# A planner that is given a duration for TensorE's changes of kind, and a preference for the kind that ran last

## The chip, the cores and the metric

The kernel runs on one core of a Trainium2 chip. Five engines work side by side, each through its own list of instructions in order: TensorE (PE in the profile; PEld is its weight load), VectorE (DVE), ScalarE (ACT), GpSimd (POOL) and SyncE (SP), which issues the DMAs. The metric is the device time of one execution in microseconds (us); lower is better.

## The reference

Three layers follow each other. Attention works on chunks of 64 tokens; its output is 2304 tokens of 512 numbers. A gated layer with an RMS norm and a layer of four experts follow.

```python
scores = scale * q_c @ k_c.T            # batch 4, 8 heads, 9 chunks of 64 x 64
attn = exp(scores - max); attn = attn / (sum(attn) + 1e-9)
x = attn @ v_c                          # -> 2304 x 512
xn = x / sqrt(mean(x * x) + 1e-6) * rms_g
x = (silu(xn @ w_gate) * (xn @ w_val)) @ w_out          # 512 -> 1536 -> 512, weights in float64
out = sum over e of p[:, e] * (relu(x @ w1[e]) @ w2[e]) # 4 experts, 512 -> 1024 -> 512
```

## The kernel before

The kernel does not issue its work in the order of the code. Each piece is added to a `Plan` as a node: the engine or engines that can do it, a duration, what it needs, which buffers it takes and gives, and a rank. `Plan.run` then makes the list: 90 passes of `forward`, which simulates the engines and always places the node that can start first (of those within 0.05 us on one engine, the one with the lower rank), and `backward`, which sets every rank to the latest start that still meets the end. When three passes bring nothing, the best ranks are taken with random noise (SEED, NOISE). The order of the best pass is written out; the planned times themselves do not reach the chip, only the order on each engine and the buffers. First ranks are made from due times, which start at `T0`; the first step of a weight conversion (`c1` in `converted`) also may not start before its rank (`after`), which is the due time less 8 us.

Tokens are in 18 tiles of 128, in blocks of 4, 4, 4, 4 and 2 tiles. `attention` does for each tile: loads of q, k and v (SyncE, L515), four TensorE transposes of q and as many of k (L552), copies to SBUF as qT and kT (ScalarE L561 or VectorE L563), the scores as 64-wide matmuls (`scores`, node s2, L582), maximum, subtraction and exponent (VectorE L601, L606, ScalarE L619), transposes of e (s3, L628), the values as 64-wide matmuls (`values`, s4, L657, into the one "av" bank), division, norm, transposes of x (s5, L716), and the split of x into a high and a low part (xh, xl). Each group of transposes has the planned duration 0.436 us and each group of 64-wide matmuls 1.2.

The gate and value weights come as float64 words in loads of 512 KB (`load_raw`, L772) and are converted by a chain that starts on ScalarE (`c1`, L792). The wide matmuls (128 x 128 x 512) of the first two weight columns (`proj`, L1141) run beside the attention of later tiles. Behind them come chains of seven products over pairs of blocks (L1287), then the output layer and the experts (L1684, L1876), with wide matmuls throughout. In `load_qkv` and `load_raw` the planned duration of an issue is 1.25 us for q, k or v and 1.6 for raw weights, and the transfer is planned at 2.2 or 2.0 us behind it.

Of the kernel before, what the change touches and what calls it, by code (L numbers as in the profile page):

```python
# [19 lines left out]
class Plan:  # L20
# [3 lines left out]


    PASSES = 90
    SEED = 10
    NOISE = 0.5
    LATENCY = 0.2
    MARGIN = 0.3  # L30

    def __init__(self):
        self.free_at = {}
# [13 lines left out]
    def add(self, eng, cost, emit, needs=(), takes=(), rank=0.0, lag=0.0, table=None, after=0.0, port=None):  # L47

        n = Node()
        n.engs = {eng: cost} if isinstance(eng, str) else eng  # L50
        n.emit, n.takes, n.rank, n.lag, n.table, n.after = emit, takes, rank, lag, table, after
        n.port = len(n.engs) > 1 and "Pool" in n.engs or eng == "Pool" if port is None else port
        n.needs = [x for x in needs if x is not None]
        n.gives = []
        n.alone = True
        n.users = []
        n.then = None
        n.end = None
        n.seq = len(self.nodes)
        n.open = len(n.needs)  # L60
        for x in n.needs:
            x.users.append(n)
        self.nodes.append(n)
        return n
# [13 lines left out]
    def run(self):  # L78


        first = {r: [list(x) for x in v] for r, v in self.res.items()}
        best, stalled = None, 0
        rng = random.Random(self.SEED)
        for k in range(self.PASSES):
            end = self.forward(first)
            stalled += 1
            if best is None or end < best[0] - 1e-6:
                best, stalled = (end, self.order, [n.rank for n in self.nodes]), 0
            if end < 1e8 and stalled < 3:
                self.backward()  # L90
            else:
                stalled = 0
                for n, r in zip(self.nodes, best[2]):
                    n.rank = r + rng.uniform(-self.NOISE, self.NOISE)
        for _, _, eng, n, ids in sorted(best[1], key=lambda x: x[:2]):
            n.ids = ids
        self.order = best[1]
        held = None
        for _, _, eng, n, ids in sorted(best[1], key=lambda x: x[:2]):
            n.emit(eng, *ids)  # L100
            if n.port and eng == "DVE":
                held = self.last()
            elif n.port and eng == "Pool" and held is not None and n.alone:
                self.behind(self.last(), held)
                held = None

    def forward(self, first):
# [1 line left out]
        self.res.update({r: [list(x) for x in v] for r, v in first.items()})  # L109
        self.state.clear()  # L110
        self.free_at, self.ready, self.order = {}, {}, []
        self.table, self.port_free, self.giver = None, 0.0, None
        for n in self.nodes:
            n.open, n.end, n.after_buffer = len(n.needs), None, []
        for n in self.nodes:
# [3 lines left out]
        while left:  # L119
            best = None  # L120
            for eng, ready in self.ready.items():
                cand = None
                for n in ready:
                    s = self.start_of(n, eng)
                    k = (s, n.rank, n.seq)
                    if cand is None:
                        cand = (k, n)
                    elif s < cand[0][0] - EPS or (s < cand[0][0] + EPS and k[1:] < cand[0][1:]):
                        cand = (k, n)
                if cand and (best is None or cand[0][0] < best[0]):  # L130
                    best = (cand[0][0], eng, cand[1])
            s, eng, n = best
            if s > 1e8:
                return 1e9
            cost = n.engs[eng]
            if n.table:
                if self.table != n.table:
                    cost += 1.28
                self.table = n.table
# [16 lines left out]
            for r, owner, k in n.gives:  # L156
                i = owner.ids[k]
                if callable(r):
                    r = r(i)
# [10 lines left out]
    def backward(self):  # L170
# [17 lines left out]
        for _, _, eng, n, _ in sorted(self.order, key=lambda x: (x[0] + x[3].cost, x[1]), reverse=True):  # L188
            t = late.get(n, end) - n.lag
# [9 lines left out]
                if x is not None:  # L199
                    late[x] = min(late.get(x, 1e9), s)  # L200
        for n in self.nodes:
            n.rank = n.late

    def make_ready(self, n):
        lat = self.MARGIN if "PE" in n.engs else self.LATENCY
# [14 lines left out]
def tile_attention_moe_moe2(  # L220
# [37 lines left out]
    NS = 6  # L258


    T0 = 36.0
    STRETCH = 1.3
    LEAD = 8.0
    HOLD = 0.0
# [266 lines left out]
    def attention(grp):  # L531
# [10 lines left out]
        for i in grp:  # L542
# [4 lines left out]
            for nm in "qk":  # L547
# [18 lines left out]
                tr = norm  # L566
                n = add("PE", 0.436, lambda e, a, b, f=transpose: f(e, a), needs=[ld[nm]], takes=["a", nm + "T"], rank=rank(i, 18))
                norm[nm, i] = n
                n.gives.append((nm, ld[nm], 0))
                c = add({"ACT": 0.6, "DVE": 0.69}, 0, copy, needs=[n], rank=rank(i, 17))  # L570
                c.gives.append(("a", n, 0))
# [16 lines left out]
                    tiles["ee", i] = at_p.tile([P, ng * H, CH], F32, tag=etag, name="e")  # L588

            s2 = add("PE", 1.2, scores, needs=[cp["q"], cp["k"]], takes=["a"] + (["e"] if i == key else []), rank=rank(i, 16))  # L590
            s2.gives += [("qT", norm["q", i], 1), ("kT", norm["k", i], 1)]
            if i == key:
                e_node = s2
# [29 lines left out]
        for n_, i in enumerate(grp):  # L623
# [8 lines left out]

            s3 = add("PE", 0.436, transpose_e, needs=[ex] + s3s, takes=["a", "eT"], rank=rank(i, 10))
            s3s.append(s3)
            if i == grp[-1]:
                s3.gives.append(("e", e_node, 1))

# [23 lines left out]
                tiles["xps", i] = ps  # L661

            s4 = add("PE", 1.2, values, needs=[ce, first[i]["v"]], takes=["av", "xs"], rank=rank(i, 8))
            s4.gives += [("eT", s3, 1), ("v", first[i]["v"], 0)]

            def total(_, i=i):
# [50 lines left out]
                tiles["xtps", i] = ps  # L717

            s5 = add("PE", 0.436, transpose_x, needs=[sl], takes=["a"], rank=rank(i, 3))
            s5.gives.append(("xs", s4, 1))  # L720

            def high(_, i=i):
# [46 lines left out]
    def load_raw(key, src, shape, dt, rank):  # L769
# [3 lines left out]
            tiles["raw", key] = t  # L773

        ld = add("SP", 1.6 if dt == I32 else 1.4, load, needs=[prev_ld[0]], takes=["raw"], rank=rank - 4, lag=2.0)
        prev_ld[0] = ld
        return ld

# [1529 lines left out]
```

## Time and profile before

| | |
|---|---|
| median of 3 runs | 1215.2 us (1212.56 to 1216.45) |
| profiled execution | 1215.69 us, span 1213.9 us |
| TensorE busy | 1196.7 us of the span (99%) |
| VectorE, ScalarE, GpSimd busy | 956.7, 593.9, 229.8 us |
| DMA | 227.00 MB, 187 GB/s on average |

The span goes from the first to the last instruction; the profiled execution's time also holds what lies around it. In the timeline a row merges instructions of one line that follow each other: start, the time up to the last one's end, line, tiles, shapes, count, and in brackets the idle time before it and what ended it. TensorE's matmuls overlap, so the pace of its groups is read from one start to the next. PEclk is the granted clock as a share of 2.4 GHz.

### The profile page before, as it was taken

What the parts mean: (1) busy time and instruction counts of PE and PEld (TensorE: products, weight loads), DVE (VectorE), ACT (ScalarE), POOL (GpSimd) and SP (SyncE); (2) the same over time, 40 slices, a digit from 0 to 9 for tenths busy, and PEclk for the clock granted to TensorE, in tenths of its full rate; (3) what the DMA queues carried; (4) which work ended last, traced back from release to release, by engine and by line L of the source; (5) the groups of instructions that cost most, each with busy time, mean ns of one, the idle gap of its engine ahead of it and who ended that gap; (6) DMA issues with size and microseconds to landing.
All of it is one profiled execution on the core that took longest, in us unless ns stands there. A gap on an engine that the chain in (4) does not pass through costs nothing.

```text
span 1213.9 us, 18543 instructions
## 1 busy us (share of the span) xinstructions
PE 1196.7 (99%) x6950; PEld 1015.5 (84%) x6950; DVE 956.7 (79%) x1416; ACT 593.9 (49%) x948; POOL 229.8 (19%) x175
## 2 busy tenths in 40 slices
PE   8899999999999999999999999999999999999998
PEld 7778888888888888888888888888788888888887
DVE  4888978888869689987888888888997466766577
ACT  5757544554647645455444444545535433342333
POOL 0132122211220021320332323323200101111001
PEclk9999999999999999999999999999999999999999
DMA  9973245545544772665465563754675755546553
GB/s 188 204 169 96 75 133 189 195 156 181 194 173 153 256 245 90 235 218 202 142 246 186 196 215 130 256 202 152 239 242 196 259 192 181 205 169 242 183 178 117
DMA packets 159662, 227.00 MB, mean 187 GB/s; under 512 B 66956, under 2 KB 102868, under 8 KB 159572
## 3 DMA queue, kind: packets, MB, share of 16 engines
q1 hardware_dynamic: 159572, 225.82, 56.1%
q8 instruction: 55, 0.90, 0.3%
q14 instruction: 35, 0.29, 0.1%
HBM read 137.66 MB, written 88.12 MB: 186 GB/s over the span
## 4 chain that ended last, share of the span: by engine, by line
PE 76%; DVE 4%; DMA 1%; ACT 0%; issue 0%; POOL 0%; SPq 0%; DVEq 0%; ACTq 0%
PE yps L1876 33%; PE hps L1684 25%; PE hps L1287 8%; PE hps L2112 4%; PE yr L2156 3%; PE hps L1416 1%; PE yo L1494 1%; DVE xa L1591 1%; DVE ha L1803 1%; PE ot L2042 1%; DMA raw<-in_moe_w_gate_dram 1%; DMA raw<-in_moe_w_val_dram 0%; DVE acc L1604 0%; DVE xx L1604 0%; DVE acc L1907 0%
## 5 line engine op out<-in xcount | busy, mean ns | idle before, releaser
L1876 PE MATMUL yps<-ha,w 128*128 128x512 f32 x1848 | 426.0, 390 | 0.6 <-DVE ha L1803 0.6
L1876 PEld LDWEIGHTS yps<-ha,w 128*128 128x128 f32 x1848 | 345.3, 188 | 72.1 <-DVE ha L1803 1.4
L1684 PE MATMUL hps<-xa,w 128*128 128x512 f32 x1344 | 313.9, 390 | 0.9 <-DVE w L946 0.6
L1684 PEld LDWEIGHTS hps<-xa,w 128*128 128x128 f32 x1344 | 250.0, 188 | 52.5 <-DVE w L946 1.0
L1803 DVE TENSOR_TENSOR ha<-hs,ha 128x1024 fp32r<-128x1024 f32 (+1 forms) x126 | 148.9, 1195 | 30.3 <-ACT ha L1797 30.0
L1797 ACT ACTIVATE ha<-hs 128x1024 fp32r<-128x1024 f32 (+1 forms) x126 | 119.2, 961 | 103.5 <-PE yps L1876 56.4
L1820 POOL TENSOR_TENSOR hs<-hs 128x1024 f32<-128x1024 f32 (+1 forms) x31 | 67.8, 2186 | 324.4 <-DVE ha L1803 284.5
L939 ACT ACTIVATE w<-raw 128x512 fp32r<-128x512 f32 x128 | 77.5, 627 | 81.4 <-DVE raw L953 30.5
L946 POOL TENSOR_TENSOR w<-raw,w 128x512 fp32r<-128x512 f32 x49 | 68.6, 1409 | 237.9 <-ACT w L939 81.2
L1907 DVE TENSOR_TENSOR acc<-acc,yps 128x512 f32<-128x512 f32 x128 | 85.1, 682 | 31.6 <-PE yps L1876 31.1
L1697 ACT ACTIVATE hps<-hps 128x512 f32<-128x512 f32 x64 | 37.3, 583 | 114.2 <-PE hps L1684 111.7
L1287 PE MATMUL hps<-xh,w 128*128 128x512 f32 x232 | 77.1, 390 | 0.0
L1890 ACT ACTIVATE yps<-yps 128x512 f32<-128x512 f32 x88 | 51.1, 581 | 44.7 <-PE yps L1876 35.3
L1745 DVE SCALAR_TENSOR_TENSOR hs<-hps,pb 128x512 f32<-128x512 f32 x96 | 64.9, 685 | 4.5 <-PE hps L1684 3.4
L1287 PE MATMUL hps<-xs,w 128*128 128x512 f32 x264 | 64.8, 389 | 0.0
L946 DVE TENSOR_TENSOR w<-raw,w 128x512 fp32r<-128x512 f32 x79 | 58.9, 767 | 5.8 <-ACT w L939 5.5
L953 DVE TENSOR_TENSOR raw<-raw 128x256 f32<-128x256 f32 x121 | 51.4, 425 | 14.2 <-POOL w L946 9.8
L1803 DVE TENSOR_TENSOR ha<-hl,ha 128x1024 fp32r<-128x1024 f32 x42 | 50.7, 1220 | 13.3 <-ACT ha L1797 13.2
L1797 ACT ACTIVATE ha<-hl 128x1024 fp32r<-128x1024 f32 x42 | 44.3, 1058 | 29.8 <-PE yps L1876 16.1
L1705 DVE TENSOR_TENSOR hps<-hps,p 128x512 f32<-128x512 f32 x32 | 22.3, 698 | 46.0 <-ACT hps L1697 46.0
L1287 PEld LDWEIGHTS hps<-xs,w 128*128 128x128 f32 x264 | 49.5, 188 | 10.4
L1287 PEld LDWEIGHTS hps<-xh,w 128*128 128x128 f32 x232 | 43.6, 188 | 8.9
(166 smaller groups left out, 1791.8 us busy)
## 6 DMA issues: line engine op xcount, KB each, us to landing
w<-wk SPq DMA_DIRECT2D x112, 512.0 KB, 4.5
wk<-w SPq DMA_DIRECT2D x110, 512.0 KB, 4.9
raw<-in_moe_w_dram SPq DMA_DIRECT2D x32, 512.0 KB, 4.8
hl<-sd SPq DMA_DIRECT2D x48, 256.0 KB, 3.1
sd<-s SPq DMA_DIRECT2D x38, 256.0 KB, 2.1
wk<-w SPq DMA_DIRECT2D x32, 256.0 KB, 2.6
w<-wk SPq DMA_DIRECT2D x32, 256.0 KB, 3.5
raw<-in_moe_w_gate_dram SPq DMA_DIRECT2D x12, 512.0 KB, 3.5
```

The costliest lines, as they stand in the source:

```text
L939: nc.scalar.activation(out=w1t[key, c][:, :, 0], in_=half(c in "DA"), func=AF.Copy)
L946: e_.tensor_tensor(out=w[:, :, 1], in0=half(c in "DA"), in1=f32(w[:, :, 0]), op=ALU.subtract)
L953: e_.tensor_tensor(out=a, in0=a, in1=b, op=ALU.add)
L1287: nc.tensor.matmul(out=bank[b], lhsT=w[:, m, wi, kk, :], rhs=xx[xi][:, kk, :], start=start and (kk, i) == (0, 0), stop=(kk, i) == (1, 2), ...
L1684: nc.tensor.matmul(out=bank[b], lhsT=w[:, m, wi, kk, :], rhs=xx[xi][:, kk, :], start=start and (kk, i) == (0, 0), stop=(kk, i) == (1, 2), ...
L1745: nc.vector.scalar_tensor_tensor(out=HT[tg, g, m][:, fp], in0=source(), scalar=0.0, in1=pb[tg, e, i], op0=ALU.max, op1=ALU.mult)
L1797: nc.scalar.activation(out=ops[tg, g][m][0][:, cuts[k]], in_=x(frm, k), func=AF.Copy)
L1803: nc.vector.tensor_tensor(out=l[:, cuts[k]], in0=x(frm, k), in1=f32(h[:, cuts[k]]), op=ALU.subtract)
L1820: e_.tensor_tensor(out=x(to, k), in0=x(one, k), in1=x(two, k), op=op)
L1876: nc.tensor.matmul(out=bank[b, d], lhsT=w[:, m, wi, d, :], rhs=hh[xi][:, fp, :], start=start and (fp, i) == (0, 0), stop=(fp, i) == (1, 2) ...
L1890: nc.scalar.activation(out=bank[to, d], in_=bank[frm, d], func=AF.Copy, scale=scale)
L1907: nc.vector.tensor_tensor(out=a, in0=a, in1=bank[b, d], op=ALU.subtract if minus else ALU.add)
```

## The change

The nodes of TensorE in the attention stage get a kind, `mode`: "t" for the four groups of transposes of a tile, "s" for its two groups of 64-wide matmuls; all others have None. In `forward`, the planned duration of a TensorE node whose kind differs from that of the node before grows by an entry of SWITCH (0.09 to 0.12 us; none for changes to None), and a node of the kind that ran last has its rank counted 0.7 lower (KEEP) when nodes tie for the earliest start. SEED goes from 10 to 3 and T0 from 36 to 26. A way to set the time of a load by hand (LOAD_AT, `fixed`) is added with an empty table.

```diff
@@ -24,10 +24,12 @@
 
 
     PASSES = 90
-    SEED = 10
+    SEED = 3
     NOISE = 0.5
     LATENCY = 0.2
     MARGIN = 0.3
+    KEEP = 0.7
+    SWITCH = {("t", "s"): 0.09, ("s", "t"): 0.12, (None, "s"): 0.1, (None, "t"): 0.1}
 
     def __init__(self):
         self.free_at = {}
@@ -54,6 +56,7 @@
         n.gives = []
         n.alone = True
         n.users = []
+        n.fixed = n.mode = None
         n.then = None
         n.end = None
         n.seq = len(self.nodes)
@@ -91,7 +94,7 @@
             else:
                 stalled = 0
                 for n, r in zip(self.nodes, best[2]):
-                    n.rank = r + rng.uniform(-self.NOISE, self.NOISE)
+                    n.rank = r + rng.uniform(-self.NOISE, self.NOISE) if n.fixed is None else n.fixed
         for _, _, eng, n, ids in sorted(best[1], key=lambda x: x[:2]):
             n.ids = ids
         self.order = best[1]
@@ -109,7 +112,7 @@
         self.res.update({r: [list(x) for x in v] for r, v in first.items()})
         self.state.clear()
         self.free_at, self.ready, self.order = {}, {}, []
-        self.table, self.port_free, self.giver = None, 0.0, None
+        self.table, self.port_free, self.giver, self.mode = None, 0.0, None, None
         for n in self.nodes:
             n.open, n.end, n.after_buffer = len(n.needs), None, []
         for n in self.nodes:
@@ -122,7 +125,7 @@
                 cand = None
                 for n in ready:
                     s = self.start_of(n, eng)
-                    k = (s, n.rank, n.seq)
+                    k = (s, n.rank - (self.KEEP if n.mode and n.mode == self.mode else 0.0), n.seq)
                     if cand is None:
                         cand = (k, n)
                     elif s < cand[0][0] - EPS or (s < cand[0][0] + EPS and k[1:] < cand[0][1:]):
@@ -133,6 +136,10 @@
             if s > 1e8:
                 return 1e9
             cost = n.engs[eng]
+            if eng == "PE":
+                if n.mode != self.mode:
+                    cost += self.SWITCH.get((self.mode, n.mode), 0.0)
+                self.mode = n.mode
             if n.table:
                 if self.table != n.table:
                     cost += 1.28
@@ -199,7 +206,7 @@
                 if x is not None:
                     late[x] = min(late.get(x, 1e9), s)
         for n in self.nodes:
-            n.rank = n.late
+            n.rank = n.late if n.fixed is None else n.fixed
 
     def make_ready(self, n):
         lat = self.MARGIN if "PE" in n.engs else self.LATENCY
@@ -258,7 +265,8 @@
     NS = 6
 
 
-    T0 = 36.0
+    T0 = 26.0
+    LOAD_AT = {}
     STRETCH = 1.3
     LEAD = 8.0
     HOLD = 0.0
@@ -566,6 +574,7 @@
                 tr = norm
                 n = add("PE", 0.436, lambda e, a, b, f=transpose: f(e, a), needs=[ld[nm]], takes=["a", nm + "T"], rank=rank(i, 18))
                 norm[nm, i] = n
+                n.mode = "t"
                 n.gives.append((nm, ld[nm], 0))
                 c = add({"ACT": 0.6, "DVE": 0.69}, 0, copy, needs=[n], rank=rank(i, 17))
                 c.gives.append(("a", n, 0))
@@ -588,6 +597,7 @@
                     tiles["ee", i] = at_p.tile([P, ng * H, CH], F32, tag=etag, name="e")
 
             s2 = add("PE", 1.2, scores, needs=[cp["q"], cp["k"]], takes=["a"] + (["e"] if i == key else []), rank=rank(i, 16))
+            s2.mode = "s"
             s2.gives += [("qT", norm["q", i], 1), ("kT", norm["k", i], 1)]
             if i == key:
                 e_node = s2
@@ -632,6 +642,7 @@
 
             s3 = add("PE", 0.436, transpose_e, needs=[ex] + s3s, takes=["a", "eT"], rank=rank(i, 10))
             s3s.append(s3)
+            s3.mode = "t"
             if i == grp[-1]:
                 s3.gives.append(("e", e_node, 1))
 
@@ -661,6 +672,7 @@
                 tiles["xps", i] = ps
 
             s4 = add("PE", 1.2, values, needs=[ce, first[i]["v"]], takes=["av", "xs"], rank=rank(i, 8))
+            s4.mode = "s"
             s4.gives += [("eT", s3, 1), ("v", first[i]["v"], 0)]
 
             def total(_, i=i):
@@ -717,6 +729,7 @@
                 tiles["xtps", i] = ps
 
             s5 = add("PE", 0.436, transpose_x, needs=[sl], takes=["a"], rank=rank(i, 3))
+            s5.mode = "t"
             s5.gives.append(("xs", s4, 1))
 
             def high(_, i=i):
@@ -773,6 +786,8 @@
             tiles["raw", key] = t
 
         ld = add("SP", 1.6 if dt == I32 else 1.4, load, needs=[prev_ld[0]], takes=["raw"], rank=rank - 4, lag=2.0)
+        if key in LOAD_AT:
+            ld.after, ld.fixed = LOAD_AT[key], -1000.0
         prev_ld[0] = ld
         return ld
 
```

## Rows read from the trace of the kernel before

**Rows 1.** The page, part 1: busy us (share), instructions of each engine.

```profile
PE 1196.7 (99%) x6950; PEld 1015.5 (84%) x6950; DVE 956.7 (79%) x1416; ACT 593.9 (49%) x948; POOL 229.8 (19%) x175
```

**Rows 2.** Windows: length; PE, PEld, DVE, ACT, POOL busy (count); clock; DMA share; GB/s.

```profile
0.00:44.00 44.00, 38.53 (x659) 34.51 (x660) 26.67 (x50) 24.84 (x48) 3.83 (x18) 1.00 0.93 193
44.00:56.00 12.00, 9.21 (x139) 7.73 (x139) 7.99 (x17) 8.22 (x17) 1.09 (x2) 0.86 0.90 200
56.00:80.00 24.00, 22.25 (x308) 18.64 (x305) 20.25 (x39) 16.68 (x32) 11.10 (x8) 1.00 0.97 195
80.00:140.00 60.00, 59.78 (x576) 49.94 (x575) 54.07 (x94) 36.08 (x65) 13.07 (x15) 1.00 0.31 96
140.00:1209.00 1069.00, 1066.71 (x5280) 904.74 (x5278) 846.98 (x1219) 507.71 (x788) 200.67 (x133) 1.00 0.55 191
```

**Rows 3.** Timeline of TensorE, first wide matmuls: start, us, line, work.

```profile
60.73 1.15 PE L657 MATMUL xps<-v,eT 64*64 64x65 f32 x32
61.80 0.50 PE L1141 MATMUL gps<-xh,w 128*128 128x512 f32 x1
62.14 0.39 PE L1141 MATMUL gps<-xl,w 128*128 128x512 f32 x1
62.37 0.40 PE L1141 MATMUL gps<-xh,w 128*128 128x512 f32 x1
62.70 1.15 PE L582 MATMUL sc<-kT,qT 64*64 64x64 f32 x32
...
75.94 0.39 PE L1141 MATMUL vps<-xh,w 128*128 128x512 f32 x1
76.17 0.60 PE L552 MATMUL tps<-ident,q 128*128 128x128 f32 x4
76.61 0.60 PE L628 MATMUL eps<-ident,e 128*128 128x128 f32 x4
...
77.40 0.48 PE L1141 MATMUL vps<-xh,w 128*128 128x512 f32 x1
77.72 0.39 PE L1141 MATMUL vps<-xl,w 128*128 128x512 f32 x1
```

**Rows 4.** Timeline of ScalarE at the first weight conversion (idle before, releaser).

```profile
45.81 0.66 ACT L792 ACTIVATE f64a<-raw 128x512 f32<-128x512 f32 x1 [3.19 <-DMA raw<-in_moe_w_gate_dram]
...
46.89 0.58 ACT L561 ACTIVATE qT<-tps 128x512 f32<-128x512 f32 x1
```

**Rows 5.** Timeline of TensorE at the same place.

```profile
47.52 1.12 PE L628 MATMUL eps<-ident,e 128*128 128x128 f32 x4 [2.39 <-ACT qT L561]
```

**Rows 6.** Windows again, right behind that wait.

```profile
47.52:51.56 4.04, 4.04 (x68) 3.64 (x69) 1.57 (x4) 2.96 (x6) 0.55 (x1) 0.60 1.02 242
```

**Rows 7.** Timeline of TensorE in the attention stage alone.

```profile
23.80 1.15 PE L657 MATMUL xps<-v,eT 64*64 64x65 f32 x32
24.88 0.66 PE L628 MATMUL eps<-ident,e 128*128 128x128 f32 x4
25.38 0.60 PE L716 MATMUL xtps<-ident,xs 128*128 128x128 f32 x4
...
40.78 0.60 PE L716 MATMUL xtps<-ident,xs 128*128 128x128 f32 x4
41.31 1.15 PE L657 MATMUL xps<-v,eT 64*64 64x65 f32 x32
42.30 1.10 PE L582 MATMUL sc<-kT,qT 64*64 64x64 f32 x32
43.33 0.66 PE L552 MATMUL tps<-ident,q 128*128 128x128 f32 x4
```

**Rows 8.** DMA issues before 39.4 us: count, KB, us to landing.

```profile
q<-in_q_dram SPq DMA_DIRECT2D x10, 256.0 KB, 4.7
```

**Rows 9.** Timeline of SyncE's queue at the first raw load.

```profile
39.42 1.27 SPq L772 DMA_DIRECT2D raw<-in_moe_w_gate_dram  x1
```

**Rows 10.** Timeline of TensorE at the first seven-product chain.

```profile
142.06 0.40 PE L1287 MATMUL hps<-xh,w 128*128 128x512 f32 x1
```

## The prediction

> **What bounds the kernel now.** I read the busy shares first, then the windows by stage, and only then the waits inside the one stage that has any. TensorE is busy 99% of the span [rows 1], so the question is where the last 1% lies. The windows answer it [rows 2]: from 140 to 1209 us, 88% of the span, TensorE is idle for 1069.00 - 1066.71 = 2.3 us in all. The open time lies ahead of 140 us: 5.5 us idle before 44, 2.8 from 44 to 56, 1.75 from 56 to 80, 0.2 from 80 to 140. That is the attention stage, which runs alone until the first wide matmul starts at 61.80 [rows 3].
>
> Two things show in it. The DMA engines are scarce beside TensorE: their share is 0.90 to 0.97 in the windows up to 80 us, and 0.31 from 80 to 140 [rows 2]. And the largest wait on TensorE is the end of a chain that starts elsewhere: ScalarE stands 3.19 us at the first step of a weight conversion, because the raw gate weights have not landed; the exponent and the qT copy queue behind that step [rows 4]. TensorE's transpose of e waits 2.39 us, until that copy [rows 5]. In the 4.04 us after it the granted clock is 0.60, so for most of them it stood at the lower of its two levels (1.2 GHz) [rows 6]. At the full clock the three groups in it would have taken 0.53 + 0.99 + 1.07 = 2.59 us (a transpose group ahead of a 64-wide one, a 64-wide one ahead of another, one ahead of other work) [rows 3, 7]. So the clock cost 1.45 us more, and this wait 2.39 + 1.45 = 3.84 us.
>
> **The change part by part.** No instruction is added or taken out: the matmuls, their tiles and their DMAs stay. What changes is the order that the planner writes for each engine.
>
> *LOAD_AT and fixed.* The dictionary is empty and fixed stays None, so these lines cost and bring nothing, with no cover needed.
>
> *The price of a change of kind.* The rows hold the real prices. Transpose groups start 0.44 us apart among themselves [rows 3]. One that is followed by a 64-wide group takes 0.53 (0.09 more); a lone 64-wide group then takes 1.07 or 1.08, and the first transpose group after it 0.50 (0.06 more); two 64-wide groups in a row take 0.99 + 1.03 = 2.02 [rows 3, 7]. A lone 64-wide group among transposes thus costs 0.09 + 1.07 + 0.06 = 1.22 us, and joining two saves 2 x 1.07 - 2.02 + 0.09 + 0.06 = 0.27. The new table charges 0.21 there, which is near. Its other entries are not. From wide to transposes it charges 0.1, where the rows show the wide matmul's own 0.23, then three transpose groups in 1.23 and a first wide matmul of 0.32: 1.23 + 0.32 - 0.23 = 1.32 = 3 x 0.44, so the change costs 0. From 64-wide to wide it charges nothing, where the first wide matmul takes 0.34 for 0.23; with 0.33 for the wide one ahead of the next 64-wide group, a lone group among wide matmuls costs 0.10 + 1.07 + 0.11 = 1.28 [rows 3]. The planner prices it at 1.30 there and at 1.41 among transposes; the chip at 1.28 and 1.22. So the table can send groups the wrong way (third rival).
>
> The Trainium skill has a rule beside this (TensorEngine Tiling (Array Packing), "Key Properties"): changing the tiling mode, not just the tile, drains TensorE. By it both sides of a 64-wide run would be charged whatever stands there, and the side between transposes and wide matmuls, both on the whole array, not at all. The rows go with the rule and against the table; by it seven joins among wide matmuls would be an estimated 7 x 0.33 = 2.3 us (0.10 + 0.11 + 2 x 1.07 - 2.02), a little over the term used here.
>
> What the preference can save: 18 score groups and 18 value groups make 36, of which three pairs stand side by side (one at 41.31 [rows 7]), so 33 runs. At best each score group stands beside a value group: 18 runs, 15 joins, 4.1 us; at least nothing changes. It decides only among instructions that can start within 0.05 us of each other and whose ranks lie within 0.7, and a value group also needs the one "av" bank. I take about half: 7 x 0.27 = 1.9 us.
>
> *The plan's pace.* Per tile the planner had 4 x 0.436 + 2 x 1.2 = 4.14 us of TensorE; the chip takes 4 x 0.44 + 2 x 1.22 = 4.20. The old 1.2 already held the changes. Charged again, a tile is up to 4.14 + 2 x 0.21 = 4.56, and over the ten tiles ahead of the first raw load the plan runs some 3.6 us slower than the chip. That works in two ways. The plan's SyncE queue sends q, k and v in 3 x 1.25 = 3.75 us a tile and stands still while their buffers are full; a raw weight load goes into the first such hole. In the kernel before, it went out at 39.42 us [rows 9], behind the loads of ten whole q tiles [rows 8]: ten times 3.75 is 37.5, so the plan had hardly a hole before that. With slower tiles the hole comes earlier, and the raw loads pass q, k and v on that one queue. That is the gain below; the loss is the first rival.
>
> *T0 from 36 to 26.* Ranks made from due times all move by the same 10 and are made anew from the plan's end after the first pass. What stays is the earliest start of each conversion: 28 us for the first key, now 18. It did not bind before: the step came at 45.81, behind a load issued at 39.42 [rows 4, 9]. For a load issued before some 24 us it would have bound, so the lower T0 opens the way. The first weights of the next stage may start at 36 + 18 x 2.72 x 1.3 - 8 = 91.7, now 81.7 us. I cost that at nothing: TensorE is busy 59.78 of the 60 us from 80 to 140 [rows 2]. With that cover gone it would fall on VectorE's queue, 54.07 busy there, and the nearest bound is the 0.2 us TensorE waits in that window now.
>
> *What an earlier gate load is worth.* It removes the 3.84 us above if ScalarE no longer waits there, or if wide matmuls stand ready to fill the wait. It moves 512 KB ahead of tile loads: at 195 GB/s [rows 2] every later q, k and v comes 2.6 us later. Lower end 0 (other loads have slack), upper end 2.6 (all of it reaches TensorE); with the DMA share so near 1 I take the middle, 1.3. Net 2.5 us. If nothing is closed it is 0; if all idle from 44 to 80 us went, it would be 2.8 + 1.75 + 1.45 = 6.0.
>
> *SEED.* It redraws the noise of the 90 passes. It can move the small waits after 140 us, 2.3 us in all [rows 2], either way; I take 0.
>
> Sum: 1.9 + 2.5 = 4.4 us. The profiled execution took 1215.69, so 1211.3; it stood 0.5 us over the median shown, so the forecast is 1215.2 - 4.4 = 1210.8 us. A difference within 0.3% (3.65 us) is about what a measurement of this kernel can't tell from no change; the forecast clears that by under one microsecond.
>
> **The rivals.** *First, slower: ScalarE waits longer.* The plan, 3.6 us slower on TensorE over ten tiles than the chip, puts the conversion's first step too early in ScalarE's queue, and the load lands when the DMA engines let it: 6.4 us from issue to use [rows 4, 9], where the plan gives 1.6 + 2.0. The 3.19 us grow by up to 3.6, TensorE's wait with them, and the low clock lasts about twice as long: 3.6 + 1.45 = 5.05, with no joins 1220.3 us. It decides once the growth passes 3.65 - 1.45 = 2.2 us. For it: the wait is there, and the plan errs to this side. Against: the slower plan also moves the load itself forward.
>
> *Second, only the joins come.* The gap stays, or returns at the next raw load. 1215.2 - 1.9 = 1213.3, the same.
>
> *Third, wrong prices.* Some 14 of the 64-wide groups go from transposes to wide neighbours at 1.28 - 1.22 = 0.06 us each, and none is joined: 1216.0, the same.
>
> *Fourth, the change doesn't do what it says.* Three joins stay three, and the new draw moves waits about to no sum: 1215.2.
>
> **How the numbers follow.** Forecast 0.45, first rival 0.15, second 0.22, third 0.08, fourth 0.10. So faster 0.45; the same 0.22 + 0.08 + 0.10 = 0.40; slower 0.15. The range runs from all joins and all idle from 44 to 80 us, 1215.2 - 4.1 - 6.0 = 1205.1, to 1218.6, which leaves out most of the first rival and little else. The likeliest case alone: 1205.1 to 1211.5.
>
> **What would show it.** Fewer than 33 runs of 64-wide work, some 26. The first raw gate load issued before 35 us, and its conversion's first step without a 3 us wait on ScalarE. The first wide matmul well ahead of 61.80. Idle from 44 to 56 us under 1 us, and no clock under 0.95 there. The first of the seven-product chains, which starts at 142.06 us now [rows 10], starts near 138, and from there the traces run alike. It is wrong if that start does not move, if the gap at 44 us only shifts to where loads were pushed back, or if waits over 1 us appear after 140 us, where nothing is to be won.

## The result, and the profile after

The changed kernel took 1220.06 us (median of 7 runs, 1218.46 to 1225.24) beside 1213.28 us for the kernel before (median of 7, 1211.41 to 1216.45). The ratio is 1.0054, with an interval of 1.0041 to 1.0068: 0.54% slower, where 0.4% faster was forecast; 1220.06 lies above the range. The profiled execution took 1218.8 us, of which the span is 1216.9.

Busy shares hardly moved (compare [rows 1]):

```profile
PE 1195.2 (98%) x6950; PEld 1014.3 (83%) x6950; DVE 965.2 (79%) x1416; ACT 594.8 (49%) x946; POOL 233.0 (19%) x179
```

The windows of [rows 2], now of the kernel after:

```profile
0.00:44.00 44.00, 37.59 (x657) 33.11 (x657) 29.42 (x56) 24.76 (x50) 4.38 (x19) 1.00 1.06 205
44.00:56.00 12.00, 10.38 (x205) 9.35 (x202) 11.23 (x23) 9.44 (x19) 2.03 (x3) 1.00 0.98 183
56.00:80.00 24.00, 20.82 (x249) 17.10 (x248) 20.66 (x38) 15.38 (x28) 6.79 (x6) 1.00 0.99 218
...
140.00:1209.00 1069.00, 1063.24 (x5243) 901.33 (x5242) 845.36 (x1205) 501.29 (x777) 204.05 (x136) 1.00 0.55 190
```

Two lines matter. TensorE's idle time from 140 us on, 2.3 us before, is 1069.00 - 1063.24 = 5.8 us. And idle time ahead of 80 us did not shrink: 6.4 + 1.6 + 3.2 = 11.2 us for 10.0 before.

The waits on TensorE from 0 to 80 us say what the idle time became there (us in total, times, longest):

```profile
PE sc L591 <- ACT kT L569: 3.3, 5, 1.1
PE xtps L728 <- DVE xs L717: 3.1, 3, 1.5
...
PE tps L560 <- DMA k<-in_k_dram: 2.0, 4, 0.7
PE tps L560 <- DMA q<-in_q_dram: 1.1, 1, 1.1
```

The 2.39 us of [rows 5] are gone. In their place stand waits for loads of k and q, 3.1 us together, and for VectorE (`xtps`), 3.1 us too.

The gate load and its conversion, on SyncE and ScalarE (compare [rows 9] and [rows 4]):

```profile
31.68 1.15 SPq L785 DMA_DIRECT2D raw<-in_moe_w_gate_dram  x1
...
37.48 0.69 ACT L807 ACTIVATE f64a<-raw 128x512 f32<-128x512 f32 x1 [2.11 <-DMA raw<-in_moe_w_gate_dram]
...
62.31 0.66 ACT L807 ACTIVATE f64a<-raw 128x512 f32<-128x512 f32 x1 [4.19 <-DMA raw<-in_moe_w_gate_dram]
```

The load goes out 7.7 us earlier. ScalarE still stands 2.11 us at the first conversion, and 4.19 us at the second one of gate weights (3.19 before).

TensorE's timeline: a joined pair, two waits for loads behind the first wide matmuls, and the start of the first seven-product chain (compare [rows 3] and [rows 10]):

```profile
12.74 1.15 PE L591 MATMUL sc<-kT,qT 64*64 64x64 f32 x32 [0.36 <-ACT kT L569]
13.72 1.10 PE L668 MATMUL xps<-v,eT 64*64 64x65 f32 x32
14.75 0.66 PE L560 MATMUL tps<-ident,q 128*128 128x128 f32 x4
...
56.27 0.48 PE L1156 MATMUL gps<-xh,w 128*128 128x512 f32 x1
...
59.61 0.63 PE L560 MATMUL tps<-ident,q 128*128 128x128 f32 x4 [1.15 <-DMA q<-in_q_dram]
60.90 0.63 PE L560 MATMUL tps<-ident,k 128*128 128x128 f32 x4 [0.66 <-DMA k<-in_k_dram]
...
139.32 0.39 PE L1302 MATMUL hps<-xh,w 128*128 128x512 f32 x1
```

Wide matmuls start at 56.27 instead of 61.80, and the chain 2.7 us earlier, although TensorE's idle time up to there grew: what it did up to there took less time. So at 139 us this execution was ahead. From that chain to the end of the span it then took 1216.9 - 139.3 = 1077.6 us, where the kernel before took 1213.9 - 142.1 = 1071.8. The loss of 5.8 us lies behind the attention stage. The waits after 80 us name one that the old list does not have:

```profile
PE yr L2171 <- DVE ap L1922: 3.0, 1, 3.0
PE hps L1302 <- ACT hps L1316: 1.0, 2, 0.6
```

### The profile page after: what moved, and what is told of

Its sections match the earlier page's. It is cut to its first block, busy times and chain, and to the rows that moved or that the text cites. A ratio compares the mean times of both kernels' runs of the same rounds, so it can differ in the third digit from the quotient of the medians.

```text
span 1216.9 us, 18562 instructions
## 1 busy us (share of the span) xinstructions
PE 1195.2 (98%) x6950; PEld 1014.3 (83%) x6950; DVE 965.2 (79%) x1416; ACT 594.8 (49%) x946; POOL 233.0 (19%) x179
## 4 chain that ended last, share of the span: by engine, by line
PE 56%; DMA 1%; DVE 0%; issue 0%; ACT 0%; SPq 0%
PE yps L1891 24%; PE hps L1699 24%; PE yr L2171 4%; PE hps L2127 4%; DMA xx<-yk 1%; PE ot L2057 1%; DVE ha L1818 0%; DVE ot L2066 0%; DVE ap L1922 0%; ACT yps L1905 0%; ACT ha L1812 0%; SPq L976 0%; SPq L907 0%; ACT xa L1602 0%
## 5 line engine op out<-in xcount | busy, mean ns | idle before, releaser
L1891 PE MATMUL yps<-ha,w 128*128 128x512 f32 x1848 | 425.9, 390 | 0.7 <-DVE ha L1818 0.7
L1891 PEld LDWEIGHTS yps<-ha,w 128*128 128x128 f32 x1848 | 345.3, 188 | 72.0 <-DVE ha L1818 1.3
L1835 POOL TENSOR_TENSOR hs<-hs 128x1024 f32<-128x1024 f32 (+1 forms) x29 | 65.3, 2250 | 327.3 <-DVE ha L1818 324.7
L961 POOL TENSOR_TENSOR w<-raw,w 128x512 fp32r<-128x512 f32 x51 | 72.1, 1424 | 215.3 <-ACT w L954 87.4
L1922 DVE TENSOR_TENSOR acc<-acc,yps 128x512 f32<-128x512 f32 x128 | 85.1, 684 | 30.8 <-PE yps L1891 30.7
L1302 PE MATMUL hps<-xh,w 128*128 128x512 f32 x224 | 75.4, 389 | 0.0
L1302 PE MATMUL hps<-xs,w 128*128 128x512 f32 x252 | 62.8, 390 | 0.0
L1302 PEld LDWEIGHTS hps<-xs,w 128*128 128x128 f32 x252 | 47.2, 188 | 10.1 <-DVE p L1336 0.4
L2171 PEld LDWEIGHTS yr<-w,hb 128*128 128x128 f32 x384 | 49.6, 197 | 4.6 <-DVE ap L1922 3.4
```

The source lines that it names most:

```text
L961: e_.tensor_tensor(out=w[:, :, 1], in0=half(c in "DA"), in1=f32(w[:, :, 0]), op=ALU.subtract)
L1302: nc.tensor.matmul(out=bank[b], lhsT=w[:, m, wi, kk, :], rhs=xx[xi][:, kk, :], start=start and (kk, i) == (0, 0), stop=(kk, i) == (1, 2), ...
L1835: e_.tensor_tensor(out=x(to, k), in0=x(one, k), in1=x(two, k), op=op)
L1891: nc.tensor.matmul(out=bank[b, d], lhsT=w[:, m, wi, d, :], rhs=hh[xi][:, fp, :], start=start and (fp, i) == (0, 0), stop=(fp, i) == (1, 2) ...
L1922: nc.vector.tensor_tensor(out=a, in0=a, in1=bank[b, d], op=ALU.subtract if minus else ALU.add)
L2171: nc.tensor.matmul(out=got["y"][:, d * 2 * P:(d + 1) * 2 * P], lhsT=hs[2 * g + f // 2][:, f % 2, xi, t * P:(t + 1) * P], rhs=w[:, f % 2, w ...
```

## The place of the loss

`ap` collects one of the seven products of the expert layer, for the first pair of token blocks. In the last group there, two additions on VectorE (L1907 before, L1922 after, in `gather`) add the last products (`yps`) to it. TensorE's next `yr` product (L2156, L2171) does not read `ap`. It takes the bank that the first `yps` stood in, and that bank comes free with the first addition: in the kernel after, that addition ends at 881.91 us and `yr` starts at 881.96. TensorE's timeline there, first of the kernel before, then of the one after:

```profile
871.87 7.73 PE L1876 MATMUL yps<-ha,w 128*128 128x512 f32 x32 [0.65 <-DVE ha L1803]
...
879.82 3.13 PE L2156 MATMUL yr<-w,hb 128*128 128x256 f32 x24 [0.21 <-DVE ap L1907]
882.79 2.91 PE L1876 MATMUL yps<-ha,w 128*128 128x512 f32 x12
```

```profile
871.31 7.65 PE L1891 MATMUL yps<-ha,w 128*128 128x512 f32 x32 [0.66 <-DVE ha L1818]
...
881.96 4.64 PE L2171 MATMUL yr<-w,hb 128*128 128x256 f32 x24 [3.00 <-DVE ap L1922]
886.44 2.91 PE L1891 MATMUL yps<-ha,w 128*128 128x512 f32 x12
```

From the first to the last of these starts the old list takes 882.79 - 871.87 = 10.92 us, the new one 15.13: 4.2 us more. Of these, 3.00 - 0.21 = 2.8 are the wait, and 4.64 - 3.13 = 1.5 are the same 24 matmuls at a lower clock. The windows from 878 to 890 us of both, with the granted clock in the third column from the right:

```profile
878.00:890.00 12.00, 11.79 (x75) 10.40 (x74) 12.00 (x18) 6.75 (x11) 1.28 (x1) 1.00 0.71 254
```

```profile
878.00:890.00 12.00, 8.99 (x48) 7.98 (x47) 9.66 (x15) 5.77 (x9) 0.00 (x0) 0.86 0.43 164
```

What VectorE does meanwhile, before and after:

```profile
878.49 0.68 DVE L1820 TENSOR_TENSOR hs<-hs 128x512 f32<-128x512 f32 x1
879.09 1.27 DVE L1907 TENSOR_TENSOR ap<-ap,yps 128x512 f32<-128x512 f32 x2
880.28 2.67 DVE L1803 TENSOR_TENSOR ha<-hs,ha 128x512 fp32r<-128x512 f32 x4
```

```profile
875.39 2.49 DVE L1818 TENSOR_TENSOR ha<-hs,ha 128x512 fp32r<-128x512 f32 x4
877.79 1.29 DVE L1835 TENSOR_TENSOR hs<-hs 128x512 f32<-128x512 f32 x2
879.00 1.29 DVE L1818 TENSOR_TENSOR ha<-hs,ha 128x512 fp32r<-128x512 f32 x2
880.62 0.69 DVE L1818 TENSOR_TENSOR ha<-hs,ha 128x512 fp32r<-128x512 f32 x1 [0.33 <-ACT ha L1812]
881.23 0.68 DVE L1922 TENSOR_TENSOR ap<-ap,yps 128x512 f32<-128x512 f32 x1
```

In the old list the additions come behind one sum (`hs`) and ahead of the next four low parts (`ha`). In the new one two sums and three low parts stand before the first addition. VectorE is idle for only 0.33 us of this, at the third low part, so it is the order that makes `yr` late.

## The experiments

Three theories stood against each other. *The draw*: the new order happens to put the two additions late, and that is the loss. *The pace*: the prices make the plan slower than the chip, its orders fit the chip less well, and that is the loss. *The loads*: what was won in the attention stage went back to q, k and v on the one queue. "Chain" is the start of the first seven-product chain in the profiled execution; "rest" is from there to the end of the span. Each ratio is to the kernel before on the same chip.

| kernel | median us | before us | ratio, 95% | chain | rest |
|---|---|---|---|---|---|
| before (first profile) | 1213.28 | | | 142.1 | 1071.8 |
| after (first profile) | 1220.06 | 1213.28 | 1.0054 [1.0041, 1.0068] | 139.3 | 1077.6 |
| before_again | 1214.69 | 1215.79 | 0.9994 [0.9984, 1.0004] | 141.2 | 1071.6 |
| after_again | 1221.28 | 1215.78 | 1.0038 [1.0023, 1.0053] | 146.2 | 1077.3 |
| e1_draw_only | 1220.46 | 1215.79 | 1.0033 [1.0020, 1.0046] | 143.4 | 1076.7 |
| e2_table_only | 1217.98 | 1215.79 | 1.0021 [1.0011, 1.0030] | 141.8 | 1073.6 |
| e3_gather_early | 1219.33 | 1215.79 | 1.0024 [1.0014, 1.0033] | 142.6 | 1074.0 |
| e7_gather_late | 1221.04 | 1215.07 | 1.0047 [1.0032, 1.0063] | 143.3 | 1076.1 |
| e4_before_rows (one run) | 1208.07 | 1215.78 | | 134.0 | 1072.2 |
| e5_after_rows (one run) | 1211.69 | 1215.78 | | 133.7 | 1076.1 |
| e6_row_prices | 1214.71 | 1215.78 | 0.9990 [0.9982, 0.9999] | 140.2 | 1071.3 |
| e8_row_prices_draw | 1213.89 | 1215.07 | 0.9990 [0.9981, 0.9998] | 139.7 | 1072.3 |
| e9_lags_only | 1218.77 | 1215.07 | 1.0032 [1.0019, 1.0045] | 145.6 | 1071.9 |
| e12_lags_only_draw | 1217.32 | 1215.32 | 1.0016 [1.0007, 1.0024] | 142.7 | 1072.8 |
| e10_table_lags | 1213.57 | 1214.92 | 0.9988 [0.9979, 0.9996] | 139.3 | 1070.7 |
| e11_table_first | 1217.05 | 1215.32 | 1.0011 [1.0002, 1.0020] | 145.3 | 1070.5 |

The rest falls into two groups. The five executions with a late addition (after, after_again, e1, e5, e7) lie at 1076.1 to 1077.6, all others at 1070.5 to 1074.0.

**The kernel before, unchanged (before_again).**

> The kernel before, unchanged, for a second profile and the spread of its executions. The theory that the 3.84 us at 44 us (the wait for the first raw weights and the half clock behind it) belongs to the list expects it in this profile too. The theory that it belongs to the one execution profiled first expects a profile without the low clock, and a time of 1211 to 1213 us. The ratio is 1.000 in both.

It gave 0.9994. The wait at the exponent came again: in its waits from 0 to 80 us the first line is

```profile
PE eps L628 <- ACT qT L561: 3.0, 2, 2.8
```

So the wait of [rows 5] belongs to the old list, not to one execution.

**The draw alone (e1_draw_only).** The kernel before with the new SEED and T0, no prices.

```diff
-    SEED = 10
+    SEED = 3
-    T0 = 36.0
+    T0 = 26.0
```

> The kernel before with SEED 3 and T0 26 alone, no price and no preference. Theory A (the loss lies in waits after 140 us that another draw of the search puts elsewhere; the prices gain about 2.4 us in the attention stage): the first seven-product chain starts at 142 us or so, 64-wide runs stay near 33, and the time differs from the kernel before by the waits after 140 us alone, up to 4 us either way. Theory B (the prices make the plan slower than the chip, and that costs the time): 1213 us, no difference from before.

It lost 0.33% with no price in the plan and 34 runs of 64-wide work (a run is a stretch of 64-wide groups with no other work between them), and had the same wait:

```profile
885.08 4.63 PE L2156 MATMUL yr<-w,hb 128*128 128x256 f32 x24 [2.93 <-DVE ap L1907]
```

The wait needs no prices. The pace theory, as the cause of the whole loss, fell here. SEED and T0 were changed together, and no run tells which of them brings the wait.

**The prices alone (e2_table_only).** The kernel after with SEED = 10 and T0 = 36.

> The changed kernel with SEED 10 and T0 36 as before: prices and preference alone. Theory A: runs of 64-wide work fall to 30 or fewer, the first chain starts near 139.5 us, waits after 140 us are those of another draw, 2 to 6 us; so 1210 to 1215 us if the two additions at 879 us stand where the kernel before has them. Theory B: 1219 to 1221 us, with waits for loads of q and k on TensorE before 80 us as in the changed kernel (3.1 us).

It has 29 runs of 64-wide work and no wait at `yr`, and loses 0.21%, about 2.2 us; those do not come from the additions. In its profile the chain starts where it did, and the rest is 1.8 to 2.0 us longer than in the two profiles of the kernel before, with other waits for VectorE, the longest 1.2 us at L1891.

e1 and e2 also tell what moves the first gate load. On SyncE, in e1 and then in e2:

```profile
47.63 1.74 SPq L772 DMA_DIRECT2D raw<-in_moe_w_gate_dram  x1
```

```profile
30.27 1.03 SPq L785 DMA_DIRECT2D raw<-in_moe_w_gate_dram  x1
```

The new SEED and T0 alone put it 8.2 us later than in [rows 9]; the prices and the preference alone put it 9.2 us earlier.

**The additions moved, both ways (e3_gather_early, e7_gather_late).** e3 is the kernel after, with the two additions put ahead of three low parts just before the list is written out. e7 is the kernel before, with the first addition put behind three low parts and the second behind a fourth. The third entry in e7 lets the `yr` product, which takes the bank, be written out behind them; its place in TensorE's order stays.

```diff
+        early = {3691: 885.58, 3693: 885.585}
+        best = (best[0], [(early.get(x[3].seq, x[0]), *x[1:]) for x in best[1]], best[2])
```

```diff
+        late_ = {3691: 884.69, 3693: 885.38, 3703: 885.39}
+        best = (best[0], [(late_.get(x[3].seq, x[0]), *x[1:]) for x in best[1]], best[2])
```

> The changed kernel with one thing moved: the two additions into ap at 881 to 883 us go back in VectorE's list to behind the sums, as in the kernel before, ahead of three low parts. Theory A: TensorE's wait of 3.0 us for them falls to 0.2 and the kernel is 2.5 to 3 us faster than the changed one, 1217 us. Theory B: the wait goes but comes back within the next products, and the time stays at 1220.

> The kernel before with the reverse of the earlier edit: the two additions into ap go behind two low parts and two sums in VectorE's list, as in the changed kernel. If that order is what costs, TensorE waits 2 to 3 us for them at 880 us and the kernel loses 2.5 to 4 us: 1.002 to 1.003. If the wait only takes the place of one that the kernel before has elsewhere (the plan of both has about 6 us idle there), the ratio is 1.000.

TensorE's timeline in e3, then in e7:

```profile
883.18 3.14 PE L2173 MATMUL yr<-w,hb 128*128 128x256 f32 x24 [0.82 <-DVE ap L1924]
```

```profile
872.97 7.77 PE L1878 MATMUL yps<-ha,w 128*128 128x512 f32 x32 [0.65 <-DVE ha L1805]
...
883.79 4.63 PE L2158 MATMUL yr<-w,hb 128*128 128x256 f32 x24 [3.06 <-DVE ap L1909]
888.26 2.91 PE L1878 MATMUL yps<-ha,w 128*128 128x512 f32 x12
```

Moved early, the wait falls from 3.00 to 0.82 us, the 24 matmuls go back to 3.14, and the rest shortens by 3.3 to 3.6 us. Moved late in the old list, wait and clock appear as in the new one, the rest grows by 4.3 to 4.5, and the kernel loses 0.47%. The order of these additions is thus shown as a cause of 3.3 to 4.5 us behind the chain's start. In the whole time e3 shows less. It took 1219.33 us, where 1217 was expected, and its 0.24% and the 0.38% of the unmoved list on the same chip have intervals that overlap; the start of the chain also differs from execution to execution, as shown next. It is not all, either: e3 still stands 0.24% above the kernel before, with a rest of 1074.0 for 1071.8 and a chain at 142.6.

**The kernel after, unchanged (after_again).**

> The changed kernel again, for a second profile. The joins are in the list, so 27 runs of 64-wide work in any case. The theory that the list gains 2.4 us in the attention stage expects the first chain near 139.3 us again. The theory that the stage goes by when the loads land expects it anywhere from 139 to 143, as the earlier kernel with the same list up to 870 us (two additions moved) had it later. The wait at 879 us is 3 us in both; 1218 to 1221 us.

The chain of the same list started at 146.2, not 139.3. The window from 56 to 80 us, and the timeline of TensorE behind 63 us:

```profile
56.00:80.00 24.00, 20.30 (x286) 17.04 (x285) 16.73 (x30) 14.03 (x26) 3.62 (x4) 0.79 0.74 168
```

```profile
63.30 0.66 PE L560 MATMUL tps<-ident,q 128*128 128x128 f32 x4 [2.01 <-DMA q<-in_q_dram]
64.81 1.09 PE L560 MATMUL tps<-ident,k 128*128 128x128 f32 x4 [0.85 <-DMA k<-in_k_dram]
...
69.29 1.97 PE L591 MATMUL sc<-kT,qT 64*64 64x64 f32 x32 [0.83 <-ACT kT L569]
```

A wait of 2.01 us for a load of q, and behind it transposes of 1.09 for 0.66 and a 64-wide group of 1.97 for 1.15: here a wait for a load did what the wait at ScalarE did in the old list. With e3, whose list is the same ahead of the additions, one list gave 139.3, 142.6 and 146.2. The 2.7 us by which the first profile was ahead at the chain are no sure gain. The old list, with e7, gave 142.1, 141.2 and 143.3.

**The loads taken out of the way (e4_before_rows, e5_after_rows).** Both kernels, with q and k read as whole rows of 512 numbers in place of eight pieces of 64. These are other data, so the attention is that of other tokens; the work on every engine is the same, and v is read as before.

```diff
+                rows = src.rearrange("b h s d -> (b h s d)").rearrange("(r h d) -> r h d", h=H, d=D)
-                    out=t[off:off + n, :, 0:D], in_=src[b, :, s:s + n, :].rearrange("h p d -> p h d")
+                    out=t[off:off + n, :, 0:D], in_=rows[i * P + off:i * P + off + n] if nm != "v" else ...
```

> The kernel before, with q and k read as whole rows of 512 numbers instead of 8 pieces of 64 numbers (other data, same sizes, same list; the output is then another one). If loads set the pace of the attention stage, they land in 3 to 4 us instead of 5, TensorE's waits for them go, and the first chain starts 2 to 4 us earlier than 142. If the list's own waits set it, it stays within 1 us of 142.

> The changed kernel with the same edit of the loads. With loads out of the way what is left of the difference in the attention stage is the list's own: 6 joins at 0.27 us, 1.6 us earlier than the kernel before with the same edit, if the prices are worth anything; nothing or later, if the plan's slower pace costs as much.

The loads of q, from issue to landing from 0 to 80 us (last column), in the kernel before and in e4:

```profile
q<-in_q_dram SPq DMA_DIRECT2D x16, 256.0 KB, 5.3
```

```profile
q<-in_q_dram SPq DMA_DIRECT2D x16, 256.0 KB, 3.8
```

The chain then starts at 134.0 in the old order and 133.7 in the new one, 5 to 12 us earlier than anywhere else: the loads bound this stage in both lists. With them out of the way the new order is ahead by 0.3 us at the chain. Why so little, the sums of the windows from 0 to 140 us show, first of e4, then of e5:

```profile
sum 140.00, PE 134.88 PEld 115.44 DVE 116.16 ACT 93.39 POOL 29.00; mean PE 33.72 PEld 28.86 DVE 29.04 ACT 23.35 POOL 7.25
```

```profile
sum 140.00, PE 133.66 PEld 115.07 DVE 122.09 ACT 95.06 POOL 28.51; mean PE 33.41 PEld 28.77 DVE 30.52 ACT 23.76 POOL 7.13
```

TensorE idles 140.00 - 134.88 = 5.1 us in e4 and 6.3 in e5. The new order idles 1.2 us more and still reaches the chain 0.3 us earlier, so its work up to there is some 1.5 us shorter. Of this, 0.4 us is only put off: three 128x256 products, 0.12 us each from start to start, stand ahead of the chain's start in e4 and behind it in e5. The other 1.1 us is what the joins gave, where six at 0.27 make 1.6. The idle time has a name in the waits of e5, which e4 does not have:

```profile
PE xtps L729 <- DVE xs L718: 1.3, 3, 0.6
```

So the joined groups save TensorE some 1.1 us, and it waits 1.3 us more for VectorE. The 0.3 us at the chain is no more than the work put off.

**Prices and landings from the rows (e6_row_prices, e8_row_prices_draw).** If the plan is out of step with the chip, a better plan should win. e6 is the kernel after, with SWITCH from the rows of [rows 3, 7] (64-wide to wide charged 0.19, wide to transposes not), 64-wide groups at 0.99, landings planned nearer to those of the profile, and the additions always placed first. e8 is e6 with SEED = 15. The edit of e6, with lines shortened by `...`:

```diff
-    SEED = 3
+    SEED = 6
-    SWITCH = {("t", "s"): 0.09, ("s", "t"): 0.12, (None, "s"): 0.1, (None, "t"): 0.1}
+    SWITCH = {("t", "s"): 0.09, ("s", "t"): 0.14, (None, "s"): 0.1, ("s", None): 0.19}
-  ... lag=2.2)      # q, k, v
+  ... lag=3.7)
-            s2 = add("PE", 1.2, scores, ...
+            s2 = add("PE", 0.99, scores, ...
-            s4 = add("PE", 1.2, values, ...
+            s4 = add("PE", 0.99, values, ...
-  ... lag=2.0)      # raw weights
+  ... lag=4.0)
+                if last and what == "p7" and tg == 0:
+                    node.fixed = -1000.0
```

> A version meant to be faster than both: prices from the rows (0.99 for a 64-wide group, changes 0.09, 0.14, 0.10 and 0.19), loads planned to land 1.5 to 2 us later, as they do, and the two additions at 879 us placed first on VectorE whenever they are ready. If late loads in the plan cost the time, TensorE's waits for loads before 80 us fall under 1.5 us and the wait at 879 us under 0.5: 2 to 5 us faster than the kernel before. If every new list is a draw whose planned end says nothing of the chip to some us, it lands anywhere within 4 us of it.

> The version with prices from the rows, later landings and the two additions first, with another seed (15 instead of 6). If that version is better by its model, this draw is as good: 0.997 to 1.000 of the kernel before. If the earlier result was the draw, it lies anywhere from 0.997 to 1.004.

Both are 0.10% faster than the kernel before, with intervals that end just under 1, and some 0.5% faster than the change as it was made. That is 1.1 and 1.2 us, not the 2 to 5 that were expected of e6. They still wait for loads, e6 2.4 us where under 1.5 was expected, and e8, from 0 to 80 us,

```profile
PE tps L560 <- DMA k<-in_k_dram: 5.1, 6, 1.3
```

**Which of the three edits does it (e9_lags_only, e12_lags_only_draw, e10_table_lags, e11_table_first).** e9 has the landings and the additions, but no prices and no preference (SWITCH = {}, KEEP = 0, T0 = 26, SEED = 10); e12 is e9 with SEED = 3. e10 is the kernel after, with its own table and SEED, plus landings and additions. e11 is the kernel after plus the additions alone.

> The later landings and the two additions first alone, with the old 1.2 us for 64-wide groups and no price and no preference (T0 26, SEED 10). If the landings are what helps in the attention stage, the first chain starts as early as with the prices from the rows (139 us) and the time is 0.997 to 1.000 of the kernel before; if the prices help, it lies 1 to 2 us above that version.

> The version with the later landings and the additions first but no price, with seed 3 instead of 10. If the lack of a price made the first one slow, it lies at 1.002 to 1.004 again, with a low clock before 80 us. If that was the draw, it lies at 0.998 to 1.001.

> The changed kernel (its table, seed 3) with the later landings and the two additions first: beside the two versions with prices from the rows this differs in the prices alone, beside the version with landings alone in having the table. If the prices from the rows are what helped, it lies with the version without prices, 1.002 to 1.004 of the kernel before. If any price for a change of kind helps, it lies with the two at 0.999. The wait at 880 us is under 1 us in both cases.

> The changed kernel with the two additions first on VectorE, planned anew, and the landings as the change has them. If the late landings of loads cost what is left after the additions (the earlier one with the additions moved by hand stood at 1.0024), it lies at 1.001 to 1.003 and TensorE waits more for loads before 80 us than with the later landings. If that rest was a draw, it lies at 0.998 to 1.000 with the others.

Landings without prices lose 0.32% and 0.16%; with the given prices they win 0.12% (e10), and with the prices of the rows 0.10% twice. So the table's wrong entries made no difference that these runs tell, and the price and the preference together are worth 0.28% (e12 to e10, with the same SEED) to 0.44% (e9 to e10) beside the later landings. Landings on top of prices and additions (e11 to e10) are worth 0.23%. They did not shorten TensorE's waits for loads, as was expected: those are 4.1 us from 0 to 80 us in both. They shortened ScalarE's waits at the conversions of the gate weights, from 0 to 80 us, in e11 and then in e10:

```profile
ACT f64a L807 <- DMA raw<-in_moe_w_gate_dram: 8.3, 2, 5.5
```

```profile
ACT f64a L807 <- DMA raw<-in_moe_w_gate_dram: 1.2, 1, 1.2
```

In e11 the longer one, 5.51 us, kept a copy of kT waiting, and with it TensorE:

```profile
65.70 1.97 PE L591 MATMUL sc<-kT,qT 64*64 64x64 f32 x32 [3.20 <-ACT kT L569]
```

With value weights counted in, ScalarE stands 5.6 to 9.9 us at raw loads before 80 us in every list planned with the old landings (e4 and e5 apart), and 0.9 to 2.9 us in the five planned with the later ones. This is not all: e9 and e12 have these waits short, too, and are slow. In e10 TensorE has no idle time from 56 to 80 us, where the kernel after has 3.2:

```profile
56.00:80.00 24.00, 24.00 (x378) 20.90 (x376) 23.42 (x44) 18.52 (x32) 12.23 (x10) 1.00 1.02 201
```

Each setting stands on one or two draws, and e9 and e12, which differ in the draw alone, lie 0.16% apart. The size of each edit is open to that extent. e10 is the best version, 1213.57 us beside 1214.92.

## Why the prediction was wrong

**The step that failed** is the *SEED* term: "It can move the small waits after 140 us, 2.3 us in all [rows 2], either way; I take 0." It took the waits that the old list has as the bound for those of a new list. But all lists are made anew behind 140 us too, and a new one can have a wait that the old one has not. It measured 1077.6 - 1071.8 = +5.8 us (5.7 in the second profiles), of which 3.3 to 4.5 are the order of two additions, by e3 and e7. The remainder is not fully named: the wait at L1302 grew from 0.3 to 1.0 us in the first profile, and 0.4 us is the work put off behind the chain's start. By e1 the new SEED and T0 bring the late additions without any price; T0 was costed at nothing as well, and the runs do not separate the two. The prediction's own mark, waits over 1 us after 140 us, shows it; no rival had it. That the slower rival's 1220.3 us lies by the measured 1220.06 is luck, since it came by another road.

By the medians the forecast was off by 6.8 + 4.4 = 11.2 us. The SEED term is 5.8 of these (5.4 without the work put off). The other 5.4 are the gain of 4.4 that did not come, and some 1 us more; by this account they lie ahead of the chain, and the next two paragraphs tell why.

**Price of a change of kind (1.9 us).** Right in the trace: 27 runs of 64-wide work instead of 33, where some 26 were expected, and a joined pair takes 14.75 - 12.74 = 2.01 us, where 2.02 was read. By the rows six joins are 1.6 us of TensorE's work; e4 and e5 show 1.1. What was missing is who is late next: with the loads out of the way 1.3 us went to waits for VectorE, and nothing was left.

**Plan's pace and earlier gate load (2.5 us).** Right in direction: the load went out at 31.68 us (before 35, as expected), by e1 and e2 through the prices and the preference and not through SEED and T0, and in the first profile the gap at 44 us and its low clock went (in the second the clock from 44 to 56 us was 0.89). The clause on the first conversion held only in part: 2.11 us were still waited there. Idle from 44 to 56 us was 1.6 us, where under 1 was expected. The price for it was taken as 1.3 us, half of what 512 KB delay the later loads. By the profiles it was too small: q and k stop TensorE for 3.1 and 3.7 us in the two profiles of the new list, and for 0.2 and 2.7 us in those of the old one. In the second profile of the new list the low clock came behind such a wait, with a mean of 0.79 from 56 to 80 us. By the chain's start the gain was 2.7 us in one execution, and a loss of 4 to 5 in another. No steady gain is left, as the prediction's second mark says (a gap that shifts to where loads were pushed back).

**LOAD_AT, T0.** The empty table did nothing. T0 alone was not tried; from 80 to 140 us TensorE stayed busy, 60.00 of 60 us, as assumed.

**First rival.** A longer wait of ScalarE at the first conversion did not come: 2.11 and 2.52 us in the two profiles, for 3.19. At the second conversion of gate weights it did, 4.19 and 6.65 us for 3.19. TensorE waited 1.07 us behind the first of these and 0.83 behind the other, so it was a small part of the loss; in e11 it was 3.20 us. **Second rival.** The joins came, but alone they gained nothing. **Third rival.** Wrong prices, 0.8 us, are not seen: e6 and e8 mended the table and match e10. **Fourth rival.** The runs of 64-wide work did fall, and the draw's waits were not about no sum.

**The skill's rule** (the Trainium skill, TensorEngine Tiling (Array Packing), "Key Properties": a change of mode drains TensorE) did not decide. No run here separates its 0.33 us a join from the rows' 0.27.

**Open:** why the search of e1 and of the kernel after settles on late additions; whether SEED or T0 does it; why one list's attention stage ends at 139.3, 142.6 or 146.2 us; and how much of the 0.2% that e2 and e3 lose is the draw.

## What to carry to other kernels

When a list of instructions is made anew, every wait in it is new: a bound taken from the old list's waits bounds nothing, and a search in planned durations can leave an instruction on a busy engine, one that makes a value or frees a bank, just late enough to stop the engine that sets the end. Look in the new trace for single waits over 1 us in stages that the change was not about, and move that one instruction by hand, in both lists, before blaming the change. A saving on TensorE in a stage whose loads are late is lent, not won: take the loads out of the way once, to see what it is worth.

## What the runs showed of the hardware

- A single wait of 3.0 us mostly cost half as much again behind it. In the kernel after, in e1 and in e7 the 24 matmuls behind such a wait took 4.64, 4.63 and 4.63 us, and 3.13 or 3.14 behind waits of 0.21 and 0.82. A wait of 2.01 us in the attention stage was also followed by the low clock. It does not always come: in e5 the wait was as long, and the matmuls took 3.13 us, at a granted clock of 1.00. What decides it is open.

```profile
876.38 3.13 PE L2172 MATMUL yr<-w,hb 128*128 128x256 f32 x24 [3.21 <-DVE ap L1923]
```

- Loads of q as whole rows of 2 KB, in place of pieces of 256 bytes, landed in 3.8 us instead of 5.3 (those of k in 3.8 instead of 4.6), and the kernel took 1208.07 us beside 1215.78, more than any order moved it on that chip; one run. The Trainium skill (DMA: Bandwidth & Descriptors, "Why small descriptors are slow (HBM only)") counts 11 cycles for a descriptor of 256 bytes, 3 of them overhead. If each piece is one descriptor and the rows have almost none of this overhead, the estimate from the page's count is 3.8 x 11 / 8 = 5.2 us; the trace agrees for q, with 5.3, and not for k, with 4.6. No run here separates this from other things that the rows change.
- One list, run twice, started its first chain 7 us apart. A gain of a few microseconds in a stage bound by loads can't be read from one execution of this kernel.
